# Two levels of the seven-product scheme in the last ten MLP blocks, and weights read twice instead of once

## The chip, the cores and the metric

The kernel runs on one core of a Trainium2 chip. The metric is the device time of one execution in microseconds (us). Engines are named as in the profile: PE is TensorE's matmul side, PEld its weight loads, DVE is VectorE, ACT is ScalarE, POOL is GpSimd, and SP issues DMAs.

## The reference

The core computes attention with a threshold and, on its result, a two-layer MLP with an exact GELU:

```python
# q, k, v: (8, 8, 576, 64) float32
scale = 1.0 / np.sqrt(q.shape[-1])
scores = scale * np.matmul(q, k.transpose(0, 1, 3, 2))
thresh = np.max(scores, axis=-1, keepdims=True) - tau
scores = np.where(scores >= thresh, scores, -1000000000.0)
scores = scores - np.max(scores, axis=-1, keepdims=True)
attn = np.exp(scores)
attn = attn / (np.sum(attn, axis=-1, keepdims=True) + 1e-09)
x = np.matmul(attn, v)            # then (B, H, S, D) -> (B*S, H*D): 4608 tokens x 512
...
h = x @ w_in                      # w_in: 512 x 2048
g = 0.5 * h * (1.0 + erf(h / sqrt(2)))
out = g @ w_out                   # w_out: 2048 x 512
```

The two weight matrices arrive as 64-bit floats: `setup_inputs` multiplies a float32 array by a 64-bit scalar. The kernel turns them into 32-bit floats on the chip.

## The kernel before

**Work and its units.** Attention is done by pairs of heads: 32 pairs, each in five steps ("slots") of up to 128 query rows. The MLP is done by blocks of 256 tokens, 18 in all. Blocks 0 to 7 ("plain", `PLAIN`) are computed as written. Their matmuls are laid into the attention slots by `fill`, which emits as many of them as a hand-set curve (`GOAL`) says. Every instruction stands in its engine's queue in the order in which the program emits it (`manual_schedule`), and an engine executes its queue in order.

**The early phase.** The first 20 slots treat the four head pairs of the first batch. In them the weights are converted as well. `load_piece` fetches one piece of 128 x 512 64-bit numbers (512 KB). `conversions` turns a piece into 32-bit floats with two ACT and three DVE instructions: L172 and L173 on ACT, L180, L182 and L184 on DVE. There are 32 pieces. `convert(ns)` emits conversion steps until their nominal lengths (the numbers after `yield`) use up the budget of the slot, 3800 from the fourth slot on. A conversion that ends fetches the next piece, so a few pieces are under way at any time: half of them land in the halves of `turned_p`, which the early phase doesn't need yet, half in free buffers of x.

**The tail.** The last ten blocks, 8 to 17, are left to the end of the program (`strassen`). They are treated two at a time ("duos"), by the scheme that computes a 2 x 2 block matrix product with seven products in place of eight. For layer one the four blocks of x are the two 256-token blocks by the two halves of the 512 inputs, and w_in is cut in 2 x 2. For layer two the four blocks of the hidden values are again the two token blocks by the two halves of the 2048 hidden values. The sums of weights that the scheme needs are built on DVE before the tail (`weights_in`, L628 to L636), the sums of x for each duo in `x_sums` (L654 to L657), and those of the hidden values in `finish_chunk` (L711 to L713). Each product of layer one is two matmuls of 256 columns; all matmuls of the tail stand on line L688 (`product`). A product that has been accumulated in a PSUM bank is copied by ACT or added by DVE to a tile in SBUF, and the next product may be accumulated on top of it in the same bank only when that has been done. Between the last chunk of layer one and the matmuls of layer two that need its sums stands a short seam; layer two of a duo keeps all its sums in PSUM over the 1024 hidden values of a half, eight matmuls to a product.

**Blocks put away.** Blocks 8 to 12 are finished before the tail begins, so `put_away` writes them to DRAM and `bring` reads them back during the tail. Blocks 13 to 17 stay in SBUF; the first duo is (13, 14). The last head pair's result is divided by the softmax sums on POOL (`divide`, L502) just as the tail begins.

Of the kernel before, what the change touches and what calls it, by code (L numbers as in the profile page):

```python
# [8 lines left out]
FP32 = mybir.dt.float32  # L9
# [9 lines left out]
def kernel(  # L19
# [28 lines left out]
    nc = tc.nc  # L48
# [22 lines left out]
    order = list(range(PLAIN + 5, N_BLK)) + AWAY  # L71
    DUOS = list(zip(order[0::2], order[1::2]))
# [6 lines left out]
    ld = ctx.enter_context(tc.tile_pool(name="ld", bufs=2))  # L79
    work = ctx.enter_context(tc.tile_pool(name="work", bufs=2))  # L80
    one = ctx.enter_context(tc.tile_pool(name="one", bufs=1))
    small = ctx.enter_context(tc.tile_pool(name="small", bufs=4))
    xg = ctx.enter_context(tc.tile_pool(name="xg", bufs=7))
    op = ctx.enter_context(tc.tile_pool(name="op", bufs=2))
    gp = ctx.enter_context(tc.tile_pool(name="gp", bufs=N_DF // 2 + 2))
    dg = ctx.enter_context(tc.tile_pool(name="dg", bufs=1))
    dram = ctx.enter_context(tc.tile_pool(name="dram", bufs=1, space=bass.MemoryType.DRAM))
    ps = ctx.enter_context(tc.tile_pool(name="ps", bufs=4, space=PSUM))

# [8 lines left out]
    q_tail = [const.tile([P, P], FP32, name=f"q_tail{i}") for i in range(4)]  # L98
    v_sb = [const.tile([P, 2, KR, D], FP32, name=f"v{i}") for i in range(4)]

    turned_p = const.tile([P, 2, 2, 4 * KR, 2 * Q], FP32, name="turned_p")
    pd = [turned_p[:, e, :, :, :].rearrange("p h b i -> p (h b i)") for e in range(2)]
    sums = [const.tile([P, Q], FP32, name=f"sums{i}") for i in range(2)]
    for t in sums:
        nc.vector.memset(t, 1.0)
    pd_tail = [const.tile([P, 4 * KR, Q], FP32, name=f"pd_tail{i}") for i in range(2)]
# [7 lines left out]
    w_in_sb = [const.tile([P, d_ff], FP32, name=f"w_in{c}") for c in range(N_DM)]  # L114
    w_out_sb = [const.tile([P, d_model], FP32, name=f"w_out{j}") for j in range(N_DF)]
# [20 lines left out]
    def load_piece(eng=nc.gpsimd):  # L136
        k = loaded[0]
        if k == len(pieces):
            return
        staged = k % 2 and k < len(pieces) - LATER  # L140
        dst, src = pieces[k]
        loaded[0] += 1
        if not wide:
            nc.sync.dma_start(dst, src)
            converted[0] += 1
            load_piece()
            return
        if staged:

            half, at = divmod(k // 2 % 4, 2)  # L150
            raw = pd[half].bitcast(U32)[:, at * 2 * PIECE:(at + 1) * 2 * PIECE]
        else:
            raw = xg.tile([P, 2 * PIECE], U32, tag="x", name="raw")
        eng.dma_start(raw, src.bitcast(U32))
        raws.append((dst, raw))

    def conversions():
# [9 lines left out]
        while raws or ahead:  # L167
            if raws:
                dst, raw = raws.pop(0)
                lo, hi = (raw.rearrange("p (f w) -> p f w", w=2)[:, :, i] for i in range(2))  # L170
                power = gp.tile([P, PIECE], U32, tag="g", name="power")
                nc.scalar.activation(power.bitcast(FP32), hi.bitcast(FP32), AF.Copy, bias=0.0, scale=2.0 ** -112)  # L172
                nc.scalar.activation(dst.bitcast(U32), lo, AF.Copy, bias=0.0, scale=2.0 ** -29)  # L173
                ahead.append((dst, hi, power))
                yield 0
            if len(ahead) == LATER and converted[0] == len(pieces) - LATER:
                yield None
            if len(ahead) == 2 or not raws:
                dst, hi, power = ahead.pop(0)
                vec.tensor_scalar(power, power, 3, 0x7FFFFFF8, op0=ALU.logical_shift_left, op1=ALU.bitwise_and)  # L180
                yield 340
                vec.scalar_tensor_tensor(power, hi, 0x80000000, power, op0=ALU.bitwise_and, op1=ALU.bitwise_or)  # L182
                yield 720
                vec.tensor_tensor(dst.bitcast(U32), power, dst.bitcast(U32), op=ALU.add)  # L184
                load_piece()
                converted[0] += 1
                yield 640
# [45 lines left out]
    def load_early(p):  # L233
        b, hp = divmod(p, HP)
        s = st[p] = {}
        for name, src in (("q", q), ("k", k)):

            pool, tag = (xg, "x") if p == 2 else (ld, name)
            t = s[name] = pool.tile([P, 2, NC + 1, D], FP32, tag=tag, name=name)
# [17 lines left out]
    def turn_qk_early(p):  # L257
# [24 lines left out]
        for j, name in enumerate("qk"):  # L282
            t = s.pop(name)
            for e in range(2):
                nc.tensor.matmul(tr[e * D:(e + 1) * D, j, 0:TAIL], lhsT=t[0:TAIL, e, NC, :],
                                 rhs=ident[0:TAIL, 0:TAIL], start=True, stop=True)
        nc.scalar.copy(kT[:, S:S + TAIL], tr[:, 1, 0:TAIL])
# [176 lines left out]
    def weigh_v(p, lo, hi):  # L464
# [16 lines left out]
        for n, o, at, size in in_blocks(b, lo, hi):  # L481
            if n not in x_blk:
                x_blk[n] = xg.tile([P, N_DM, TOK], FP32, tag="x", name="x")
# [59 lines left out]
    def block_steps(n):  # L543
# [3 lines left out]
        for j in range(N_DF):  # L547
# [8 lines left out]
            if j % 2:  # L556
                late.append((g, j, hT))
                gelus(lag[0])
        for m in range(TOK // P):
# [42 lines left out]
    HF = d_ff // 2  # L602
    NJ = HF // P
    HD = d_model // 2
    NK = HD // P
    U = 512
    vec = nc.vector

    def units(t):
        flat = t.rearrange("p a b -> p (a b)") if len(t.shape) == 3 else t.rearrange("p a b c -> p (a b c)")  # L610
        return [flat[:, k * U:(k + 1) * U] for k in range(flat.shape[1] // U)]

    def unit(pool, tag, n=1):
        t = pool.tile([P, n, U], FP32, tag=tag, name="unit")
        return [t[:, k, :] for k in range(n)]

    def weights_in():

        room = [x for tag in ("q", "k", "qT", "kT") for _ in range(2) for x in unit(ld, tag)]
        room += unit(work, "p", 2) + unit(work, "p", 2)  # L620
        x_ext = [units(v_sb[i % 4])[0].rearrange("p (c t) -> p c t", c=NK) for i in range(NP - 4, NP - 1)]
        s1, s2, s4 = ({} for _ in range(3))
# [338 lines left out]
```

## Time and profile before

| | before |
|---|---|
| median of 3 runs | 1383.6 us (1381.98 to 1385.34) |
| the profiled execution's own time | 1385.34 us |
| its span, first to last instruction | 1383.6 us |
| mean granted TensorE clock | 0.994 |
| busy: PE, PEld, DVE, ACT, POOL | 1363.2, 970.0, 884.1, 654.1, 413.7 us |
| tail: first matmul of L688 to the end of the last | about 892.9 to 1380.5 us |

The profiled execution takes 1.7 us more outside its span, and it is the slowest of the three runs, 1.7 us over the median. Busy time is the time in which an engine has an instruction in work; matmuls overlap their neighbours, so PE's busy share says little of how well it is used. The chain of waits follows back from the last instruction to whatever released each step.

### The profile page before, as it was taken

The numbers are of one execution on the slowest core, as the hardware profiler recorded it, in microseconds if no ns is written. First come the engines' busy times: TensorE is split into PE (matmuls) and PEld (weight loads), VectorE is DVE, ScalarE is ACT, GpSimd is POOL, SyncE is SP. The second block draws the span as 40 slices with busy tenths as digits, with TensorE's granted clock in tenths as the row PEclk, the third lists the DMA queues.
The fourth block names the chain that finished last, engine by engine and source line by source line (L and its number), as shares of the span: only waits on it lengthen the run. The fifth ranks groups of instructions, "written<-read, shape, count | busy, mean of one in ns | idle before, by whom it ended". The sixth has DMA issues, their size and how long they took to land.

```text
span 1383.6 us, 20244 instructions
## 1 busy us (share of the span) xinstructions
PE 1363.2 (99%) x6734; PEld 970.0 (70%) x6734; DVE 884.1 (64%) x1707; ACT 654.1 (47%) x1192; POOL 413.7 (30%) x864
## 2 busy tenths in 40 slices
PE   8899999999999999999999999999999999999999
PEld 6577557466466466466476475588888888888887
DVE  6987677788888888888888888764142232241330
ACT  7886537457457448358367366241140230330420
POOL 4331344455555554554555551100000000000000
PEclk9999999999999999999999999999999999999999
DMA  9741266667777777787787776500000001001000
GB/s 273 193 143 34 66 153 150 143 152 180 152 172 183 156 189 177 158 202 175 160 207 167 165 186 122 112 0 8 23 1 24 22 1 46 16 0 54 9 8 23
DMA packets 212406, 152.43 MB, mean 110 GB/s; under 512 B 113664, under 2 KB 198976, under 8 KB 212304
## 3 DMA queue, kind: packets, MB, share of 16 engines
q1 hardware_dynamic: 191040, 112.84, 36.0%
q0 software_dynamic: 20832, 38.01, 9.8%
q8 instruction: 55, 0.90, 0.3%
q14 instruction: 47, 0.39, 0.1%
q10 hardware_dynamic: 432, 0.30, 0.1%
HBM read 55.97 MB, written 12.52 MB: 49 GB/s over the span
## 4 chain that ended last, share of the span: by engine, by line
PE 95%; DVE 2%; ACT 2%; issue 1%; DVEq 0%; ACTq 0%
PE bank L688 35%; PE o_ps L568 17%; PE hT L554 16%; PE sc L362 13%; PE xT L479 11%; PE tr L304 2%; DVE power L182 1%; DVE nmx L374 1%; ACT p L377 0%; DVE p L393 0%; ACT power L172 0%; DVE power L180 0%; ACT pT L312 0%; PE idle L122 0%; ACT diag L407 0%
## 5 line engine op out<-in xcount | busy, mean ns | idle before, releaser
L377 ACT ACTIVATE p<-sc,nmx 128x576 f32<-128x576 f32 x288 | 202.1, 738 | 273.0 <-DVE nmx L374 272.9
L393 DVE SCALAR_TENSOR_TENSOR p<-sc,thr,p 128x576 f32<-128x576 f32 x288 | 225.3, 816 | 60.5 <-ACT p L377 58.9
L374 DVE TENSOR_REDUCE nmx<-sc 128x1 f32<-128x576 f32 x288 | 205.6, 751 | 72.4 <-PE sc L362 71.7
L554 PE MATMUL hT<-x,w_in 128*128 128x256 f32 x1024 | 241.1, 385 | 0.0
L568 PE MATMUL o_ps<-w_out,g 128*128 128x512 f32 x512 | 239.0, 608 | 0.0
L554 PEld LDWEIGHTS hT<-x,w_in 128*128 128x128 f32 x1024 | 189.5, 190 | 49.2 <-issue 23.5
L375 POOL TENSOR_SCALAR thr<-nmx,tau_eff 128x1 f32<-128x1 f32 x288 | 87.8, 305 | 407.2 <-DVE nmx L374 406.2
L568 PEld LDWEIGHTS o_ps<-w_out,g 128*128 128x128 f32 x512 | 93.9, 191 | 112.0 <-issue 110.4
L479 PE MATMUL xT<-pT,v 128*64 128x256 f32 (+1 forms) x1280 | 163.8, 409 | 0.1
L362 PE MATMUL sc<-kT,qT 64*128 64x288 f32 x960 | 157.6, 433 | 3.2 <-DVE p L393 2.6
L440 DVE STREAM_TRANSPOSE turned_p<-p 128x1152 f32<-128x1152 f32 x112 | 154.4, 1378 | 3.9
L362 PEld LDWEIGHTS sc<-kT,qT 64*128 64x128 f32 x960 | 90.1, 188 | 76.6 <-issue 64.4
L479 PEld LDWEIGHTS xT<-pT,v 128*64 128x64 f32 x1280 | 89.1, 137 | 72.2 <-issue 13.6
L688 PE MATMUL bank<-x,w_in 128*128 128x256 f32 x480 | 116.7, 379 | 0.0
L688 PE MATMUL bank<-w_out,unit 128*128 128x256 f32 x520 | 115.5, 379 | 0.0
L229 POOL DMA_DIRECT2D v<-in_v_dram x208 | 110.8, 536 | 4.6 <-issue 2.7
L688 PEld LDWEIGHTS bank<-w_out,unit 128*128 128x128 f32 x520 | 98.8, 190 | 13.4
L688 PEld LDWEIGHTS bank<-x,w_in 128*128 128x128 f32 x480 | 91.2, 190 | 12.8 <-issue 0.5
L688 PE MATMUL bank<-v,unit 128*128 128x256 f32 x320 | 82.1, 379 | 0.0
L220 POOL DMA_DIRECT2D q<-in_q_dram x104 | 70.8, 686 | 8.5 <-issue 8.1
L688 PE MATMUL bank<-unit,turned_p 128*128 128x256 f32 x320 | 73.1, 379 | 0.0
L540 ACT ACT_TABLE_LOAD x56 | 71.8, 1283 | 1.0
(156 smaller groups left out, 1476.2 us busy)
## 6 DMA issues: line engine op xcount, KB each, us to landing
pT<-turned_p SPq DMA_DIRECT2D x448, 160.0 KB, 3.6
pT<-pd_tail SPq DMA_DIRECT2D x112, 80.0 KB, 2.9
q<-in_q_dram POOLq DMA_DIRECT2D x104, 72.0 KB, 3.4
k<-in_k_dram POOLq DMA_DIRECT2D x104, 72.0 KB, 2.9
inv<-turned SPq DMA_DIRECT2D x56, 128.0 KB, 3.9
v<-in_v_dram POOLq DMA_DIRECT2D x156, 40.0 KB, 3.2
x<-x SPq DMA_DIRECT2D x10, 512.0 KB, 4.4
raw<-in_moe_w_out_dram POOLq DMA_DIRECT2D x9, 512.0 KB, 4.1
```

Source lines behind the costliest of these rows:

```text
L229: eng.dma_start(t[r:P:4, e, 0:n, :], rows[:, r * KR:r * KR + n, :])
L362: nc.tensor.matmul(sc[e][:, h, 0:HALF], lhsT=lhsT, rhs=s["kT"][rows, at:at + HALF], start=True, stop=True)
L374: nc.vector.tensor_reduce(nmx[:, e:e + 1], sc, axis=AXIS.XY, op=ALU.max, negate=True)
L375: nc.gpsimd.tensor_scalar(thr[:, e:e + 1], nmx[:, e:e + 1], -1.0, tau_eff, op0=ALU.mult, op1=ALU.subtract)
L377: nc.scalar.activation(w[:, e * S:(e + 1) * S].rearrange("p (h s) -> p h s", h=2), sc, AF.Exp, bias=nmx[:, e:e + 1], scale=1.0)
L393: nc.vector.scalar_tensor_tensor(row, sc[e][:, :, 0:HALF], thr[:, e:e + 1], row, op0=ALU.is_ge, op1=ALU.mult, accum_out=den[e])
L440: nc.vector.transpose(turned_p[:, :, i // 2, 0:NB, i % 2 * Q:(i % 2 + 1) * Q], w.rearrange("p (e b i) -> p e b i", e=2, i=Q))
L479: nc.tensor.matmul(to, lhsT=s["v"][:, e, c, :], rhs=rhs, start=(c == 0), stop=(c == KR - 1))
L540: nc.scalar.activation(warm[:, 1:2], warm[:, 0:1], AF.Exp)
L554: nc.tensor.matmul(hT[:, j % 2, :], lhsT=w_in_sb[c][:, j * P:(j + 1) * P], rhs=x_blk[n][:, c, :], start=(c == 0), stop=(c == N_DM - 1))
L568: nc.tensor.matmul(o[:, 0:d_model], lhsT=g[j][:, m * P:(m + 1) * P], rhs=w_out_sb[j], start=(j == 0), stop=(j == N_DF - 1))
L688: nc.tensor.matmul(to, lhsT=l, rhs=r, start=start and k == 0, stop=k == len(pairs) - 1, skip_group_check=not start)
```

## The change

**Tail.** The ten blocks are treated in two groups of five, 1280 tokens at a time. Layer one applies the seven-product scheme twice, one inside the other: every one of the seven outer products (a quarter of w_in's sums by a quarter of x's sums) is itself seven products of 128 inputs, 128 hidden values and 320 tokens, one matmul of 320 columns each. That makes 49 matmuls for one chunk of 512 hidden values, and there are four chunks (`NJ = 4`). Layer two stays one level deep, and is computed for each chunk as soon as that chunk's hidden values are there; its result is added up in SBUF over the four chunks. The sums that the inner level needs are built for each chunk on POOL, beside the matmuls; the sums of x come on DVE and POOL.

**Conversion.** A piece is fetched twice, the second time shifted by three bytes, and converted by one ACT and four DVE instructions. Two pieces rather than four are fetched at the start, and one rather than two in each of two later places. The nominal lengths add up to 2100 a piece where they added up to 1700.

**Storage.** x's seven buffers, w_in and w_out become one tile each, and the pools are closed and reopened so that the tail's tiles take the place of attention's.

The core of the diff:

```diff
             if raws:
-                dst, raw = raws.pop(0)
-                lo, hi = (raw.rearrange("p (f w) -> p f w", w=2)[:, :, i] for i in range(2))
+                dst, raw, shifted, slots = raws.pop(0)
+                hi = raw.rearrange("p (f w) -> p f w", w=2)[:, :, 1]
+                top = shifted.rearrange("p (f w) -> p f w", w=2)[:, :, 0]
                 power = gp.tile([P, PIECE], U32, tag="g", name="power")
-                nc.scalar.activation(power.bitcast(FP32), hi.bitcast(FP32), AF.Copy, bias=0.0, scale=2.0 ** -112)
-                nc.scalar.activation(dst.bitcast(U32), lo, AF.Copy, bias=0.0, scale=2.0 ** -29)
-                yield 0
+                vec.tensor_scalar(power, hi, 0x7FF00000, None, op0=ALU.bitwise_and)
+                nc.scalar.activation(power, power, AF.Relu, bias=rebias, scale=8.0)
+                yield 340
...
-                vec.tensor_scalar(power, power, 3, 0x7FFFFFF8, op0=ALU.logical_shift_left, op1=ALU.bitwise_and)
+                vec.tensor_scalar(mant, top, 0x0FFFFFFF, 0x10000000, op0=ALU.bitwise_and, op1=ALU.bitwise_or)
                 yield 340
                 vec.scalar_tensor_tensor(power, hi, 0x80000000, power, op0=ALU.bitwise_and, op1=ALU.bitwise_or)
                 yield 720
-                vec.tensor_tensor(dst.bitcast(U32), power, dst.bitcast(U32), op=ALU.add)
+                vec.scalar_tensor_tensor(dst, mant, 2.0 ** -28, power.bitcast(FP32), op0=ALU.mult, op1=ALU.mult)
                 load_piece()
-                yield 640
+                yield 700
...
         eng.dma_start(raw, src.bitcast(U32))
+        n = 8 * PIECE - 4
+        eng.dma_start(shifted.bitcast(U8)[:, 0:n], src.bitcast(U8)[:, 3:3 + n])
...
+    def taken(to, x, first):
+        if first is None:
+            nc.scalar.copy(to, x)
+        else:
+            add(vec, to, first, x)
+    def step(which):
+        if which is not None:
+            which()
+        if beside:
+            beside.pop(0)[1]()
+        while beside and beside[0][0] is pool:
+            beside.pop(0)[1]()
+    def chain(n, m, takes, done=None, runs=1):
+        x, y = bank("sc", n), bank("mm", n)
+        v = bank("mm", n) if "m2" in m else None
...
+        before = waiting.pop(0) if waiting else (None, None)
+        step(one_of("m1", x, True))
+        step(before[0])
+        step(one_of("m7", y, True))
+        if v is not None:
+            step(one_of("m2", v, True))
+        step(before[1])
+        step(one_of("m6", x, False))
+        step(one_of("m4", y, False))
+        waiting.append((one_of("m5", x, False), one_of("m3", x, False)))
...
+        R, U, V, W, T = c[:, 0], c[:, 1], c[:, 2], c[:, 3], g[:, 0]
+            takes = {"m1": [at(0, 0)], "m7": [at(1, 1)], "m6": [at(1, 0)], "m4": [at(1, 0, True)],
+                     "m2": [at(0, 0, True)], "m5": [at(1, 1, True)], "m3": [at(0, 1)]}
...
+        def m5_all():
+            m5_out(0, 1)()
+            add(pool, flat(U), flat(U), flat(T))
+        def sums(t):
+            g11, g21, g12, g22 = (z[:, :, t, :] for z in (R, U, V, W))
+            sub_first = g[:, 0, :, t, :], g[:, 1, :, t, :]
+            add(vec, sub_first[0], g21, g22)
+            sub(vec, sub_first[1], sub_first[0], g11)
+            sub(vec, g21, g11, g21)
+        outer("a11", "b11", R, None)
+        outer("s1", "t1", T, None)
+        between()
+        outer("s2", "t2", U, R)
+        outer("s3", "t3", V, U, when(m2=m5_out(0, 0), m4=m5_out(1, 0), m5=m5_out(1, 1), m3=m5_all))
+        outer("a12", "b21", R, R, when(m3=lambda: (gelu_on(flat(W)), gelu_on(flat(R)))))
+        outer("a22", "t4", V, V, when(m3=lambda: gelu_on(flat(V))))
+        last = {"m2": lambda: gelu_on(U[:, 0, 0, :]), "m4": lambda: (gelu_on(U[:, 1, 0, :]), sums(0)),
+                "m5": lambda: gelu_on(U[:, 1, 1, :]), "m3": lambda: (gelu_on(U[:, 0, 1, :]), sums(1))}
+        outer("s4", "b22", U, U, when(**last))
+    def layer_out(blocks, j, between):
...
+        before = waiting.pop(0)
+        for m in range(MT):
+            v = bank("mm", HD)
+            def run(m=m, v=v):
+                product(v, rows(g12, m, w(1, 0)), True)
+                taken(lo[m][:, 0:HD], v, None if first else lo[m][:, 0:HD])
+            step(run)
+            if m < 2:
+                step(before[m])
+        between(-1)
+        beside.insert(0, (vec, lambda: sub(vec, g12, g12, gs2)))
+        for m in range(MT):
...
+            chain(HD, ms, takes, done)
+            between(m)
+    def last_blocks():
+        x_tiles()
+        beside.extend(x_sums())
+        for _ in range(9):
+            beside.pop(0)[1]()
+        w_out_sums(pool, 0)
...
+                if m == -1:
+                    if after[0] != n:
+                        for b, x in enumerate(GROUPS[after[0]]):
+                            nc.sync.dma_start(xall[:, b, :, :], away.pop(x))
+                    w_in_sums(pool, after[1])
+                if m == 1 and after[0] != n:
+                    beside.extend(x_sums())
```

In it, `x`, `y` and `v` are PSUM banks, two buffers for `x` and four shared by `y` and `v`; `g11`, `g21`, `g12` and `g22` of layer two are R, U, V and W, and `gs1`, `gs2` the two halves of `g`. `HD` is 256, `MT` is 5, and `w_in_sums` is 16 POOL instructions over 5632 columns for a chunk, run on DVE for the very first chunk. `x_sums` is 28 subtractions of 320 columns and four, the outer ones, of 1280.

## The prediction, made before the result was known

> **What bounds the kernel now.** I read the page first: busy shares and the chain that ended last.
>
> ```profile
> PE 1363.2 (99%) x6734; PEld 970.0 (70%) x6734; DVE 884.1 (64%) x1707; ACT 654.1 (47%) x1192; POOL 413.7 (30%) x864
> PE bank L688 35%; PE o_ps L568 17%; PE hT L554 16%; PE sc L362 13%; PE xT L479 11%; PE tr L304 2%; DVE power L182 1%; DVE nmx L374 1%; ACT p L377 0%; DVE p L393 0%; ACT power L172 0%; DVE power L180 0%; ACT pT L312 0%; PE idle L122 0%; ACT diag L407 0%
> ```
>
> PE carries the chain; the tail (L688) is 35% of it. Busy time by stretches shows two stages with different limits.
>
> ```profile
> 35.00:70.00 35.00, 28.38 (x200) 20.66 (x200) 32.96 (x70) 31.17 (x66) 13.38 (x26) 0.90 0.69 192
> 105.00:140.00 35.00, 34.51 (x212) 26.36 (x213) 24.73 (x54) 23.68 (x53) 6.10 (x17) 1.00 0.17 32
> 1000.00:1100.00 100.00, 99.48 (x462) 87.25 (x461) 29.37 (x70) 26.08 (x67) 0.00 (x0) 1.00 0.05 16
> ```
>
> Columns: the stretch, its length, then PE, PEld, DVE, ACT, POOL busy with instructions, granted clock, DMA share, GB/s. Around 50 us DVE is full (33.0 of 35), the only place where the weight conversion can matter. In the tail PE is full and DVE 29% busy: there a matmul saved is time saved, as long as its results are taken from PSUM in time. The chain in order of time prices the matmuls.
>
> ```profile
> 349.18 3.63 PE o_ps L568 x8
> 450.86 4.49 PE o_ps L568 x10
> 725.34 3.65 PE hT L554 x16
> 801.35 4.08 PE hT L554 x18
> 941.08 96.97 PE bank L688 x448
> ```
>
> A float32 matmul is two records. Two more records of 512 columns cost 0.86 us, of 256 columns 0.43. One matmul is thus 0.432 at 256 (96.97/224 agrees), 0.86 at 512, and, on the line between, 0.538 at 320. From the groups by shape come the other prices (last numbers: busy us, mean ns).
>
> ```profile
> L735 DVE TENSOR_TENSOR v<-v,bank 128x256 f32<-128x256 f32 x10 | 4.2, 421 | 3.7 <-PE bank L688 3.7
> L629 DVE TENSOR_TENSOR unit<-unit,w_in 128x512 f32<-128x512 f32 x4 | 2.8, 691 | 0.1
> L527 ACT ACTIVATE g<-g 128x512 f32<-128x512 f32 x6 | 3.2, 618 | 0.0
> L739 ACT ACTIVATE turned_p<-turned_p 128x256 f32<-128x256 f32 x10 | 4.2, 416 | 4.5 <-DVE turned_p L738 4.5
> L502 POOL TENSOR_TENSOR x<-x,inv 128x256 f32<-128x256 f32 x40 | 28.6, 728 | 0.0
> L502 POOL TENSOR_TENSOR x<-x,inv 128x128 f32<-128x128 f32 x16 | 7.3, 457 | 0.0
> L180 DVE TENSOR_SCALAR power<-power 128x512 uint32<-128x512 uint32 x32 | 13.5, 421 | 6.2 <-ACT power L172 6.2
> ```
>
> On straight lines a DVE add takes 0.49 at 320 columns, 0.82 at 640, 1.49 at 1280. The next one starts 0.08 before its end if independent, 0.04 to 0.08 after it if it needs the result (starts in the timeline). A GELU takes 0.47 at 320 and about 1.2 at 1280; POOL takes 0.86, 1.27 and 2.9 at 320, 512 and 1280. The timeline (start, length, idle before and what ended it) prices a product that must wait for a bank.
>
> ```profile
> 1038.08 0.42 DVE L738 TENSOR_TENSOR turned_p<-turned_p,bank 128x256 f32<-128x256 f32 x1 [0.44 <-PE bank L688]
> 1038.56 1.13 PE L688 MATMUL bank<-x,unit 128*128 128x256 f32 x4 [0.52 <-DVE turned_p L738]
> ```
>
> DVE starts 0.2 after the last column, PE 0.06 after DVE's end, and the first record then takes 0.1 longer (1.13 us for four where others show 1.03). Five such seams, one a duo, cost 0.8 each, 3.9 in all: 1120 x 0.432 + 3.9 = 487.7, the tail's measured 487.5.
>
> **Matmuls saved.** Layer one falls from 7 x 2 x 8 x 5 = 560 matmuls of 256 columns (241.9 us) to 49 x 4 x 2 = 392 of 320 (210.9): **31.0 us less**. Layer two keeps 14 x 5 x 4 x 2 = 560 of 256. The tail without stalls is 452.8.
>
> **Stalls in each chunk.** In the middle of a chunk DVE keeps up: one add of 0.41 to 0.49 for each product of 0.538. At the seam it doesn't. I walk the three queues from the end of product m4 of the last outer product s4 (t = 0), the time in us, for a chunk that isn't its group's first:
>
> - ACT: the GELU of V waits for m3 of the outer product before (its matmul ends at -1.08, DVE's add at -0.4) and runs to 0.85. PE's next product, v of m = 0, reads V and starts at 0.91. **Idle 0.91.**
> - The GELU of U's (1,0) ends at 1.38. DVE has already started on `sums(0)`, which stands next in its queue and waits for that: 1.42 to 3.8 (three adds of 640). Only then come v's add (4.15) and that of m5 (4.56). PE finished m5 and the second v at 3.28 and may accumulate m3 into m5's bank at 4.62. **Idle 1.34.**
> - m3 is added by 5.96, its GELU ends at 6.49, `sums(1)` at 8.9, three adds of v at 9.95, that of layer two's first m1 at 10.29. PE ended m7 at 9.58 and starts m6 in m1's bank at 10.35. **Idle 0.78.**
> - V minus gs2 (1280 columns) runs to 11.7, m7's add to 12.04; PE, done at 11.32, starts m4 at 12.10. **Idle 0.78.** From here DVE has one add of 0.34 for each 0.86.
>
> With 0.1 for each restart that is 4.2 us. In a group's first chunk ACT takes the v's, and only the first idle and 1.0 of the second are left: 2.1. Together 6 x 4.2 + 2 x 2.1 = **29.4**.
>
> **Stalls at the ends.** At the start w_in's sums (5632 columns at 1.04 ns and 16 starts of 0.11: 7.7 us from 879.8) and the first nine sums of x keep DVE until PE ends the plain blocks at 892.9, as L628 to L657 did; m1 has nothing to wait for. But `t3` is POOL's, behind the division (to 894.7) and four adds of w_out (5.0) and takes 2.9: 902.6. DVE reaches its sums of t3 at 900 with m5's add behind them, and PE waits 6.3. Between the groups x's sums delay two more products, 2.1, if the five blocks return within 12 us (2.6 MB; 273 GB/s in the first slice gives 9.6 plus some 2). The last m3 waits for m5: 0.8. The last store is two DMAs, not one: 0.4. **9.6** together.
>
> **POOL beside DVE.** In the trace of before, POOL's small add at L396 takes 0.24 alone and 0.89 beside a DVE instruction with two SBUF inputs, which keeps its 0.69 (timeline again):
>
> ```profile
> 12.37 0.24 POOL L396 TENSOR_SCALAR den<-den 128x2 f32<-128x2 f32 x1 [1.50 <-DVE p L393]
> 52.35 0.89 POOL L396 TENSOR_SCALAR den<-den 128x2 f32<-128x2 f32 x1 [1.41 <-DVE p L393]
> 52.18 0.69 DVE L184 CUSTOM_DVE_ANT_0 w_in<-power,w_in 128x1024 uint16<-128x1024 uint16 x1
> ```
>
> So I let POOL be the one that waits. Its sums for the next chunk (5632 columns, 14 us) have 30 us of layer two to hide in, even at twice the time; only the first t3 is exposed: 2 us more. DVE slowed in return is not seen: I take 0, and one POOL add of about 1 us before each of four DVE sums, 8 x 4 = 32, as the other end.
> The Trainium skill's page "GPSIMD Engine Reference" (Specifications) says POOL's SBUF interfaces are shared with DVE, in contention with DVE instructions "in a 2-port perf mode or with two SBUF inputs". It speaks against moving sums to POOL beside `sums(1)`; it doesn't say who waits. The rows show POOL waiting; by the rule read the other way the sum would be that other end.
>
> **Conversion.** DVE per piece now: L180, L182, L184 start 0.45, 0.72 and 0.61 apart, 1.79. After: two masks at 0.35 (if their strided inputs run like L180; 0.61 if like L182), 0.61 and 0.73: 2.04 to 2.56. A slot's budget of 3800 holds 2.2 pieces before (4.0 us) and 1.8 after (3.7 to 4.6). Around 50 us a slot lasts 6.8, full of DVE; over 12 such slots that is -3.6 to +8. The rest of the pieces falls where DVE has room (24.7 of 35 busy). ACT sheds a 0.68 us instruction a piece. DMA: 1.8 MB a slot of 6.8 us is 266 GB/s beside q, k and v, where 273 GB/s made the DMAs 90% busy in the first slice; waits of up to 6 are possible, and DVE's softmax stands behind a late piece. I take **+1**, ends -4 and +14.
>
> **Sum.** Against the profiled execution's own 1385.3: tail 452.8 + 29.4 + 9.2 = 491.4 against 487.5, +3.9; store +0.4; t3 +2; conversion +1: 1392.6. The median of the runs is 1.7 lower: **1391**, 0.5% slower.
>
> **Rivals.**
> - *DVE keeps up at the seam* (faster). The walk hangs on queue order and three extrapolated lengths. For it: DVE needs some 22 of the 26 us of layer one, so the work fits on the average. Against it: the order is fixed, and DVE waits for ACT ahead of PE's adds. Without the 29.4 the time is 1362. The sign turns when a chunk's stalls average below 2.7 in place of 3.7. Chance 0.22.
> - *DVE held by POOL at the seam* (slower): the other end above, 1391 + 32 = 1423 in full, half of it 1407. For it: no row has a long POOL add beside such a sum. Against it: the 0.69 beside L396. Chance 0.13.
> - *The conversion binds*: +14 in place of +1, 1404. For it the DMA share, against it the smaller budget. Chance 0.15.
> - *The sums don't run beside the products*: if products wait for writers of other parts of the same large tile (x, c), PE waits for POOL's 25 us a chunk; a fifth of it is 40 us, over 1430. No row speaks for it. Chance 0.05.
>
> **How the numbers follow.** Forecast 0.45. 0.2% (2.8 us) is about what a measurement can tell from no change. Faster: nearly all of the first rival, 0.20, and 0.03 of the forecast's lower edge. Same: 0.10, from the forecast. Slower: 0.67. The range leaves out the deeper half of the first rival and most of the second and fourth: 1372 to 1412. The forecast's own range is 1382 to 1400.
>
> **What would show it.** Right: no more idle in layer one's middle than 0.1 a product; PE idle behind "ACT" before a v product (0.9), behind DVE before m3 (1.3), m6 and m4 (0.8 each) in chunks two to four; 320-column matmuls 0.538 apart; the tail 491 long; its start near 893. Wrong: two-input DVE sums longer than 0.82, the tail's start later than 897, or DVE level at m3.

## The result and the profile after

| | before | after |
|---|---|---|
| median of the runs | 1384.0 us (1382.0 to 1385.3) | 1432.7 us (1431.6 to 1434.2) |
| the profiled execution's own time, its span | 1385.3, 1383.6 | 1431.6, 1429.8 |
| tail: first matmul to the end of the last | 892.9 to 1380.5 = 487.5 | 888.1 to 1425.1 = 537.1 |
| matmul time of the tail at full pace | 483.8 | 452.8 |
| PE's time over that pace | 3.7 | 84.3 |

The changed kernel takes 1.0354 times as long, with an interval of 1.0336 to 1.0372; forecast were 1391 us, with a range of 1372 to 1412. The last row is the difference of the two above it. Where a wait is priced "over the pace" below, the spacing of the tail's matmul records is set against the nominal one (0.216 at 256 columns, 0.270 at 320): whatever is over it is waiting or a slow clock. The matmuls shrank by 31.0 us as forecast. The time over the pace grew by some 80.

The page of the kernel after, first the busy times, then the chain by line:

```profile
PE 1353.3 (95%) x6398; PEld 911.7 (64%) x6398; DVE 1106.9 (77%) x2040; ACT 600.2 (42%) x1000; POOL 683.4 (48%) x1106
PE bank L781 27%; PE o_ps L611 16%; PE hT L596 14%; PE sc L403 12%; PE xT L520 10%; DVE c L663 2%; DVE g L663 2%; ACT c L834 1%; DVE o L666 1%; PE tr L345 1%; DVE g L666 1%; DVE x L663 1%; DVE c L666 1%; DVE p L434 1%; DVE nmx L415 1%
```

The tail's matmuls now stand on L781, and behind them the chain has DVE's sums (L663, L666), which it didn't have before. The same stretches as in the prediction, with the same columns:

```profile
35.00:70.00 35.00, 30.31 (x216) 22.20 (x215) 34.24 (x76) 25.48 (x52) 18.50 (x35) 0.95 1.04 324
1000.00:1100.00 100.00, 92.62 (x383) 73.69 (x382) 64.38 (x123) 10.80 (x20) 38.68 (x34) 0.97 0.00 1
```

In the tail DVE went from 29% to 64% busy, POOL from nothing to 39%, and PE from 99% to 93% at a clock of 0.97. Around 50 us it is the other way round: PE got busier. The groups of DVE's instructions in the tail say where to look (last numbers: busy us, mean ns of one):

```profile
L666 DVE TENSOR_TENSOR c<-c,bank 128x320 f32<-128x320 f32 x304 | 147.3, 487 | 40.0 <-PE bank L781 27.1
L663 DVE TENSOR_TENSOR g<-g,c 128x640 f32<-128x640 f32 x16 | 26.5, 1655 | 0.6
L663 DVE TENSOR_TENSOR c<-c 128x640 f32<-128x640 f32 x16 | 24.2, 1511 | 0.0
L663 DVE TENSOR_TENSOR c<-c,g 128x1280 f32<-128x1280 f32 x8 | 15.0, 1880 | 0.0
```

An add of a bank to a tile takes the 0.49 that the line through before's rows gave. An add of 640 columns with both inputs in SBUF takes 1.66 and 1.51 in place of 0.82. That was the first sign under "Wrong" in the prediction. The timeline of DVE and POOL at one seam shows why (start, length, idle before):

```profile
1057.95 1.78 DVE L663 TENSOR_TENSOR g<-g,c 128x640 f32<-128x640 f32 x1
1059.65 1.88 DVE L663 TENSOR_TENSOR c<-c 128x640 f32<-128x640 f32 x1
...
1057.19 1.85 POOL L663 TENSOR_TENSOR s_out<-w_in,s_out 128x512 f32<-128x512 f32 x1
1059.12 1.73 POOL L666 TENSOR_TENSOR s_in<-s_out 128x512 f32<-128x512 f32 x1
1060.92 1.73 POOL L663 TENSOR_TENSOR s_in<-s_in,s_out 128x512 f32<-128x512 f32 x1
```

The two engines take turns. DVE's sum starts while POOL's is under way and ends 0.7 us after POOL's end; POOL's next starts in the middle of DVE's and is stretched in its turn, from 1.27 to 1.73. A still plainer pair stands at the change of groups, where some 0.45 us of DVE's work stood beside one long instruction of POOL:

```profile
1149.69 3.07 DVE L663 TENSOR_TENSOR x<-t_x 128x320 f32<-128x320 f32 x1
...
1149.52 2.88 POOL L663 TENSOR_TENSOR xall<-xall 128x1280 f32<-128x1280 f32 x1 [14.30 <-DMA out_dram<-o]
```

What that does to PE, at the same seam:

```profile
1062.31 0.81 PE L781 MATMUL bank<-xall,s_in 128*128 128x320 f32 x2 [3.06 <-DVE c L666]
1062.95 5.30 PE L781 MATMUL bank<-w_out,c 128*128 128x256 f32 x16
1068.09 1.03 PE L781 MATMUL bank<-t_out,c 128*128 128x256 f32 x4
1069.66 1.13 PE L781 MATMUL bank<-t_out,g 128*128 128x256 f32 x4 [0.54 <-DVE o L666]
1071.97 1.13 PE L781 MATMUL bank<-t_out,c 128*128 128x256 f32 x4 [1.18 <-DVE o L666]
```

The lines with idle time are m3, m6 and m4. m3 waits 3.06 us, and the sixteen records behind it take 5.30 us: the granted clock is 0.5 for 3.4 us. The last chunk has no sums of a next chunk beside it, and is a control that the kernel brings with it:

```profile
1393.38 0.81 PE L781 MATMUL bank<-xall,s_in 128*128 128x320 f32 x2 [1.01 <-DVE c L666]
1394.02 3.62 PE L781 MATMUL bank<-w_out,c 128*128 128x256 f32 x16
1397.48 1.03 PE L781 MATMUL bank<-t_out,c 128*128 128x256 f32 x4
1399.05 1.13 PE L781 MATMUL bank<-t_out,g 128*128 128x256 f32 x4 [0.54 <-DVE o L666]
1400.78 1.13 PE L781 MATMUL bank<-t_out,c 128*128 128x256 f32 x4 [0.60 <-DVE o L666]
```

There the waits are those of the walk: by the spacing 1.13 (the v product), 1.27, 0.81 and 0.87 us, where the walk, with 0.1 for each restart, had 1.01, 1.44, 0.88 and 0.88. The two other long waits stand at the tail's start and between the groups, both behind DVE:

```profile
904.95 1.44 PE L781 MATMUL bank<-xall,s_plain 128*128 128x320 f32 x2 [11.89 <-DVE c L666]
1154.21 1.13 PE L781 MATMUL bank<-w_out,c 128*128 128x256 f32 x4 [3.18 <-DVE o L666]
```

### The profile page after: what moved, and what is told of

It is laid out like the page before. It is cut to its first block, busy times and chain, and to the rows that moved or that the text cites. A ratio compares the mean times of both kernels' runs of the same rounds, so it can differ in the third digit from the quotient of the medians.

```text
span 1429.8 us, 20064 instructions
## 1 busy us (share of the span) xinstructions
PE 1353.3 (95%) x6398; PEld 911.7 (64%) x6398; DVE 1106.9 (77%) x2040; ACT 600.2 (42%) x1000; POOL 683.4 (48%) x1106
## 4 chain that ended last, share of the span: by engine, by line
PE 80%; DVE 12%; ACT 3%; DMA 2%; issue 1%; SPq 1%; POOL 0%; ACTq 0%; DVEq 0%; POOLq 0%
PE bank L781 27%; PE o_ps L611 16%; PE hT L596 14%; PE sc L403 12%; PE xT L520 10%; DVE c L663 2%; DVE g L663 2%; ACT c L834 1%; DVE o L666 1%; PE tr L345 1%; DVE g L666 1%; DVE x L663 1%; DVE c L666 1%; DVE p L434 1%; DVE nmx L415 1%
## 5 line engine op out<-in xcount | busy, mean ns | idle before, releaser
L415 DVE TENSOR_REDUCE nmx<-sc 128x1 f32<-128x576 f32 x288 | 205.5, 750 | 62.5 <-PE sc L403 61.7
L596 PE MATMUL hT<-xall,w_in 128*128 128x256 f32 x1024 | 241.1, 385 | 0.0
L596 PEld LDWEIGHTS hT<-xall,w_in 128*128 128x128 f32 x1024 | 189.5, 190 | 49.2 <-issue 23.9
L666 DVE TENSOR_TENSOR o<-o,bank 128x256 f32<-128x256 f32 x240 | 98.4, 418 | 106.8 <-PE bank L781 105.8
L666 DVE TENSOR_TENSOR c<-c,bank 128x320 f32<-128x320 f32 x304 | 147.3, 487 | 40.0 <-PE bank L781 27.1
L781 PE MATMUL bank<-w_out,c 128*128 128x256 f32 x480 | 131.7, 409 | 12.0 <-ACT c L834 6.9
L781 PEld LDWEIGHTS bank<-w_out,c 128*128 128x128 f32 x480 | 98.3, 207 | 35.9 <-ACT c L834 10.9
L834 ACT ACTIVATE c<-c 128x320 f32<-128x320 f32 (+1 forms) x56 | 44.6, 811 | 141.4 <-DVE c L666 73.1
L792 ACT COPY c<-bank 128x320 f32<-128x320 f32 x32 | 13.6, 426 | 196.9 <-PE bank L781 196.8
L663 POOL TENSOR_TENSOR t_out<-w_out 128x512 f32<-128x512 f32 x16 | 21.5, 1345 | 146.2 <-PE bank L781 146.2
L781 PE MATMUL bank<-t_out,c 128*128 128x256 f32 x320 | 84.9, 389 | 6.5 <-DVE o L666 6.5
```

What stands on the lines that cost most here:

```text
L415: nc.vector.tensor_reduce(nmx[:, e:e + 1], sc, axis=AXIS.XY, op=ALU.max, negate=True)
L596: nc.tensor.matmul(hT[:, j % 2, :], lhsT=w_in_sb[c][:, j * P:(j + 1) * P], rhs=x_blk[n][:, c, :], start=(c == 0), stop=(c == N_DM - 1))
L663: eng.tensor_tensor(out, a, b, op=ALU.subtract)
L666: eng.tensor_tensor(out, a, b, op=ALU.add)
L781: nc.tensor.matmul(to, lhsT=l, rhs=r, start=start and k == 0, stop=k == len(pairs) - 1, skip_group_check=not start)
```

## The experiments

The first theory was: DVE's two-input sums are held by POOL's, and PE's long waits bring a half clock that costs as much again. The rivals: DVE simply has too much work at the seam; or the start and the change of groups carry the loss. Gains are read against the median of 1432.7. The cuts of the edits are shortened, and comments in them are for the reader.

**e1 and e2: POOL's sums away from the seam.** In e1 POOL's sums for the next chunk wait until `V` minus `gs2` is done:

```diff
-                if m == -1: ... w_in_sums(pool, after[1])
+                if m == 0:
+                    pool.tensor_copy(tail["sp"][:, 0, 0, 0:1], tail["c"][:, 2, 0, 0, 0:1])
+                    w_in_sums(pool, after[1])
```

> The kernel after, but POOL's sums of w_in for the next chunk start only when DVE has taken gs2 from V (POOL first copies one column of V). Theory H (a DVE instruction with two SBUF inputs waits until POOL's running add ends, and the other way round): the three-add sums at the seam return from 1.5 to 1.7 us an add to 0.82, every seam looks like that of the last chunk, which has no POOL sums beside it (1.0, 1.2, 0.7, 0.8 us idle), no idle reaches 3 us, and the half clock behind the seams is gone: about 4 us less in each of seven chunks, some 28 us, 1404. Rival S (the sums are slow because their operands lie in strides of 320 columns): the adds keep 1.5 us and more, time within 5 us of 1433. A third way: POOL's 20 us end too late for the next chunk and part of the gain goes there.

In e2 the same 16 sums are done by DVE, one behind each product, and POOL has none:

```diff
-                    w_in_sums(pool, after[1])
+                    w_in_sums(Later(), after[1])     # each op: beside.append((vec, op))
```

> The kernel after, but the 16 sums of w_in for the next chunk go to DVE, one behind each of 16 products of layer two, and POOL has none. Theory H: seams as in the last chunk, 1404 as in the run with POOL held; DVE has 0.5 us free for each product of 0.86 there and the sums take 0.2 to 0.7, so a few tenths of idle a chunk at most. Rival S: the seams stay as they were, and DVE has 8 us more to do in each chunk: 1433 or more.

Measured: 1405.9 us (1.0151 of before, 1.0136 to 1.0166) and 1405.6 (1.0147, 1.0130 to 1.0165). The groups of e1:

```profile
L663 DVE TENSOR_TENSOR g<-g,c 128x640 f32<-128x640 f32 x16 | 13.2, 825 | 0.6
L663 DVE TENSOR_TENSOR c<-c 128x640 f32<-128x640 f32 x16 | 13.1, 817 | 0.0
L663 DVE TENSOR_TENSOR c<-c,g 128x1280 f32<-128x1280 f32 x8 | 11.9, 1481 | 0.0
```

The sums are back at 0.82 and 1.48, and the eight seams (over the nominal pace) fall from 61.7 to 28.7 us. The median falls by 27: the profiled execution of e1 has its tail's start 4.8 us later than that of the kernel after, and its change of groups takes 3 more. Two opposite ways to part the engines give the same time, so neither the work nor its place on POOL is the cause, but that both run at once. In e2 DVE did these 16 sums of each chunk on top of its own at 3 us more in the seams than e1 and 2 less between the groups; it has room.

**e3: the conversion alone**, put into the kernel before.

> The kernel before, with the conversion of the kernel after (two fetches a piece, one ACT and four DVE instructions, two pieces fetched at the start) and nothing else of the change. The kernel after stands 9 us ahead of the one before at 400 us. Theory: that is the conversion, which takes 0.7 us less of ACT and no more of DVE in each full slot; time 1375. Rival: it comes of the other storage of x and the pools, or the ends of the early phase move and are lost again by the curve that lays out the MLP; time 1384.

1380.0 us, 0.9971 of before (0.9959 to 0.9982): the conversion gains 4.5 us, between the two values.

**e12: the ACT instruction put back into e3**, to see why it gains.

```diff
                 nc.scalar.activation(power, power, AF.Relu, bias=rebias, scale=8.0)
+                lo = raw.rearrange("p (f w) -> p f w", w=2)[:, :, 0]
+                nc.scalar.activation(dst.bitcast(U32), lo, AF.Copy, bias=0.0, scale=2.0 ** -29)
```

> The kernel of e3 (the one before with only the new conversion, 1380.0), with the second ACT instruction of a piece put back (0.68 us, 32 times; what it writes is overwritten by DVE's mask). Theory (the conversion gains because ACT is the engine that PE waits for around 50 us: PE's waits for ACT's diag fell from 7.7 to 5.3 us and the half-clock windows from five to two): the time goes back to that of before, 1384 or a little more, and PE waits for ACT's diag 7 us or more. Rival (the gain comes from fewer pieces fetched at once or from another share of the slots): 1380, as e3.

1384.5 us, 1.0007 of before (0.9994 to 1.0019): all of the gain is gone. The stretch around 50 us, first of e3, then of e12 (that of before is in the prediction: DVE 32.96, ACT 31.17):

```profile
35.00:70.00 35.00, 28.64 (x209) 20.88 (x207) 33.00 (x76) 24.63 (x52) 17.86 (x34) 0.90 1.01 307
```

```profile
35.00:70.00 35.00, 28.31 (x198) 19.97 (x199) 32.06 (x72) 29.99 (x62) 17.30 (x34) 0.90 1.01 299
```

DVE is about equally full in all three, and ACT goes 31.2, 24.6, 30.0. So the gain hangs on the second ACT instruction of a piece. Whether by ACT's load or by DVE's mask, which in e12 has to wait for that instruction because both write the same tile, this run doesn't tell. Through which waits it reaches PE is no clearer: PE waited 6.4 us for ACT's `diag` in e3, 7.3 in e12 and 7.7 before (the 5.3 of the expectation is that of the kernel after), and e12 has 13.6 us at half clock where e3 has 6.8.

**e4: a clock test**, in the kernel before: 0, 2, 4, 7 and 10 extra DVE copies at its five seams, so that PE idles for graded times.

```diff
+                if j == NJ - 1:
+                    for _ in range((0, 2, 4, 7, 10)[sb]):
+                        vec.tensor_copy(gs1(j), x)
```

> The kernel before, with 0, 2, 4, 7 and 10 extra DVE copies out of the waiting bank at the five seams between layer one and layer two, so that PE is idle there for about 0.8, 1.4, 2.1, 3.2 and 4.2 us. Theory C (an idle of PE of about 3 us brings half the TensorE clock for some 3.4 us): matmul records 0.42 apart in place of 0.216 behind the fourth and fifth seam only, 1.7 us lost behind each; time about 1384 + 8 + 3.4 = 1395. Rival (the half clock in the kernel after comes of its load, or of POOL and DVE at work, and not of the idle): records 0.216 apart behind every seam, 1392.

1397.2 us (one run). PE's timeline at the third and the fourth seam:

```profile
1136.86 1.13 PE L688 MATMUL bank<-x,unit 128*128 128x256 f32 x4 [2.22 <-DVE turned_p L742]
1137.83 1.46 PE L688 MATMUL bank<-w_out,unit 128*128 128x256 f32 x6
```

```profile
1237.42 1.34 PE L688 MATMUL bank<-x,unit 128*128 128x256 f32 x4 [3.60 <-DVE turned_p L742]
1238.56 4.71 PE L688 MATMUL bank<-w_out,unit 128*128 128x256 f32 x14
```

Behind 2.22 us of idling six records take 1.46; behind 3.60 fourteen take 4.71, some of them twice as long as the rest: 1.5 us more than fourteen at full pace. The longest wait, 5.1 us, has the same behind it. So in this kernel idling does bring the half clock (other runs, at the end of this document, say when), and one spell of it costs up to 1.7 (5.30 against 3.62 for sixteen records at after's seam).

**e5 and e9: PE kept running through m3's wait** by five spare matmuls of 256 columns. The lines are those of e9; e5 writes to `tail["other"]` in place of `nxt`.

```diff
+            if m == 1:
+                for _ in range(5):
+                    nc.tensor.matmul(nxt, lhsT=w_out_sb[0][:, 0:P], rhs=w_out_sb[0][:, 0:HD], start=True, ...)
```

> The kernel after, with five spare matmuls of 256 columns (2.16 us, into an unused half of a PSUM bank, never read) put in front of the product m3 that waits 3.2 us at each seam of layer one. No other instruction moves. Theory (after an idle time of about 3 us PE runs at half clock for 3.4 us): the wait falls to about 1 us, the half-clock windows behind the eight seams go (30.7 us at half, 15 us of work lost), 1432.7 - 15 = about 1418. Rival (the records 0.42 apart are a price of the adds that hold the seam, not of PE's idling): the spare matmuls change nothing, 1433.

1465.5 us (1.0590, 1.0573 to 1.0608): no test of the clock. The spare matmuls went into the other half of a bank tile that DVE still had to read, waited 2.8 to 3.1 us for it, and then ran their 2.2 to 3.6 us on top.

> As e5, but the five spare matmuls of each seam go into the bank that the third v product of layer two overwrites next, so that they wait for nothing that DVE still has to do (in e5 they waited 2.8 us for DVE themselves and added their own time). Theory (half clock follows an idle time of about 3 us): the wait of m3 falls from 3.2 to about 1, the half-clock windows behind the seams go, about 1418. Rival (the 0.42 apart belong to the adds and not to PE's idling): no gain, 1433 or more.

1442.1 us (1.0425, 1.0410 to 1.0439). Here they did what they were meant to; PE's timeline at one seam:

```profile
997.11 2.32 PE L920 MATMUL bank<-w_out 128*128 128x256 f32 x10
1000.35 0.81 PE L781 MATMUL bank<-xall,s_in 128*128 128x320 f32 x2 [0.92 <-DVE c L666]
1000.99 3.62 PE L781 MATMUL bank<-w_out,c 128*128 128x256 f32 x16
1004.44 1.03 PE L781 MATMUL bank<-t_out,c 128*128 128x256 f32 x4
1007.71 1.13 PE L781 MATMUL bank<-t_out,g 128*128 128x256 f32 x4 [2.24 <-DVE o L666]
1010.01 2.07 PE L781 MATMUL bank<-t_out,c 128*128 128x256 f32 x4 [1.17 <-DVE o L666]
```

m3 waits 0.92, and the sixteen records behind it run at full pace (3.62). But m6 now waits 2.24 where it waited 0.54: PE comes 1.7 us earlier to the same add, which DVE ends no sooner. Counted from the seam's first v product, m6 and m4 start at 12.97 and 15.27 us here, and at 12.95 and 15.26 at after's seam shown above (1056.71). The half clock behind m3 had thus cost nothing there; DVE's queue covered it. The second half of the first theory falls. The kernel became slower because the long idle time now lies before m6 and m4, and the half clock behind m4, where no wait for DVE covers it: this seam takes 11.3 us over the pace where it took 8.4, and the eight together some 69 in place of 61.7. The trace of after has one such seam by itself, at 1324 to 1340 us: full pace behind m3, m6 waiting 2.24, half clock behind m4, 11.4 us in all.

**e6: the start**, on e1. `t3` on DVE, `t4` behind the sums of `t3`, POOL's sums of w_out behind its sums of x.

```diff
-        yield from outer(pool, part["b12"], part["b22"], part["b12"])
-        yield from outer(vec, t4, part["b21"], t2)
...
-        yield from inner(vec, "t2", t2)
+        yield from inner(vec, "t2", t2, True)
+        yield from outer(vec, part["b12"], part["b22"], part["b12"])
         yield from inner(vec, "t3", part["b12"])
+        yield from outer(vec, t4, part["b21"], t2)
...
```

> The kernel with POOL's sums held back at the seam (1405.9), and with the sums of x in another order: t3 on DVE behind the sums of t2, t4 behind those of t3, and POOL's four sums of w_out for the first chunk behind its sums of x. Theory (PE's 11.9 us at the tail's start and its 9 us at the change of groups are DVE standing behind POOL's adds and behind t3, and 6.9 and 1.7 of them half clock behind the idle): the start falls to 5 to 8 us of short waits with no half clock, the change of groups to about 4: about 1389. Rival (DVE and POOL simply have more sums there than PE leaves time for): 1400 or more.

1395.3 us (1.0080, 1.0065 to 1.0095). The change of groups fell from 10.1 to 4.5 us over the pace, as expected, but the start only from 14.2 to 10.6, in two waits of 4.6 and 2.6 us, each still with half clock behind it. (The expectation counted 6.9 us of half clock at the start; by the spacing it was 2.5.)

**e7: the seam's order**, on e1. `a22` ahead of `a12`, each GELU as soon as its sum is there, `sums(0)` behind the adds of v and m5, the second half's sums one at every second product.

```diff
-        outer("a12", "b21", R, R, when(m3=lambda: (gelu_on(flat(W)), gelu_on(flat(R)))))
-        outer("a22", "t4", V, V, when(m3=lambda: gelu_on(flat(V))))
+        outer("a22", "t4", V, V, when(m4=lambda: gelu_on(flat(W)), m3=lambda: gelu_on(flat(V))))
+        outer("a12", "b21", R, R, when(m3=lambda: gelu_on(flat(R))))
...
-                "m4": lambda: (gelu_on(U[:, 1, 0, :]), sums(0)), "m5": lambda: gelu_on(U[:, 1, 1, :]),
-                "m3": lambda: (gelu_on(U[:, 0, 1, :]), sums(1))
+                "m4": lambda: gelu_on(U[:, 1, 0, :]), "m5": lambda: (gelu_on(U[:, 1, 1, :]), sums0()),
+                "m3": lambda: gelu_on(U[:, 0, 1, :])      # sums(1): beside, one op, one empty step
```

> The kernel with POOL's sums held back (until V minus gs2, as there), and with another order at the seam: the outer product a22 (V) before a12 (R), so that V and W have their GELU early; sums(0) behind the adds of v and m5; the second half's sums and V minus gs2 in two halves, one of them at every second product of layer two. Nothing is removed. Theory (the 3.65 us of each seam are the order of ACT's and DVE's queues): nearly all of them go, 7 x 3.65 + 2 = about 27 less than 1405.9, 1379. Rival (DVE has no room there, the waits only move to later products): 1395 or more.

1382.5 us (0.9993, 0.9981 to 1.0005). PE's seam, and a stretch of windows, of e7:

```profile
1043.86 1.03 PE L781 MATMUL bank<-w_out,c 128*128 128x256 f32 x4
1044.72 0.70 PE L781 MATMUL bank<-xall,s_in 128*128 128x320 f32 x2
1045.26 1.03 PE L781 MATMUL bank<-w_out,c 128*128 128x256 f32 x4
1046.12 0.70 PE L781 MATMUL bank<-xall,s_in 128*128 128x320 f32 x2
1046.66 3.62 PE L781 MATMUL bank<-w_out,c 128*128 128x256 f32 x16
```

```profile
985.00:1035.00 50.00, 50.00 (x214) 40.19 (x213) 32.69 (x71) 6.44 (x13) 22.27 (x24) 1.00 0.00 1
```

No idle time is left there: the eight seams together are 4 us over the pace in place of 28.7. It is the same work in another order; only one subtraction of 1280 columns a chunk is cut in two. A part came back elsewhere: the change of groups takes about 13 us over the pace in place of e1's 10.1, and the start 15.1 in place of 14.2.

**e8, e10, e11: everything together**, with the blocks' buffers chosen so that ACT doesn't copy into one whose write to memory is under way (it waited for two, 3.0 and 2.5 us, near 605 and 709).

> The two changes of order together, with sums held back, and with buffers for blocks 9 to 15 chosen so that none is used while it is still being written to memory (3.0 and 2.5 us of PE waiting near 606 and 709 us, with some half clock). Theory: the savings add up, 17 + 27 + 4 from 1405.9: about 1358, below both kernels. Rival (one stage's slack is the other's cover): over 1370.

1379.9 us (0.9971, 0.9961 to 0.9982) where 1358 was expected: the start kept 14.1 us and the change of groups about 10. PE waits twice at the start, 4.5 us up to 900 (DVE's add stands behind sums of x that waited for the division) and 5.2 us up to 920. POOL's timeline shows what is ahead of the second:

```profile
903.20 0.86 POOL L665 TENSOR_TENSOR xall<-xall 128x320 f32<-128x320 f32 x1 [9.60 <-DVE t_x L665]
```

POOL's sums of `b21` overwrite what `t4` reads, and `t4` had moved to the end of DVE's queue, so POOL idled 9.6 us and was then late for its adds for W, for which DVE waits 5.9 us. In e10 the order is mended:

```diff
+        w_out_sums(pool, 0)                # in weights_first, before the last division
...
+        yield from rest(7 if at_start else 0)
         yield from outer(vec, t2, part["b22"], t1)
         yield from outer(vec, t4, part["b21"], t2)
+        yield from inner(pool, "b21", part["b21"])
+        yield from inner(pool, "t4", t4)
...
+        yield from rest(15 if at_start else 0)
+        yield from inner(pool, "b22", part["b22"])
```

> As e8, with the tail's start in yet another order: the first chunk's sums of w_out on POOL ahead of the last division, where POOL idles 16 us; no sums of x in DVE's queue during the first outer product; t4 ahead of the sums of t2; POOL's sums of b21 and t4 behind t4, those of b22 after its adds for W and U. In e8 PE waited 4.7 us at 895 (DVE's sums of x, queued ahead of its adds, stood behind the division) and 5.4 us at 914 (POOL's sums, queued ahead of its adds for W, stood behind t4, whose input they overwrite), each with half clock behind it. Theory: both go, to 2 to 4 us of short waits: 1380 - 13 = about 1367. Rival (the work of the start doesn't fit beside 26 us of PE): 1376 or more.

1372.2 us (0.9922, 0.9908 to 0.9937); the start is down to 8.2. e11 adds empty steps behind `t2`, `t4` and `t3`:

> As e10, with the sums of x spread out further: t1 ahead of the sums of b11, an empty step behind each of t2, t4 and t3, and t4 behind the sums of t2. In e10 PE still waited 4.5 us at 897 (DVE's add for T behind t2, t4 and two sums beside POOL's) and 3.6 us at 1116 (DVE's sums beside POOL's sums of w_in), each with half clock behind it. Theory (DVE's adds come late because two or more sums of 1280 columns stand ahead of one add): the wait at 897 falls under 2 us, and the half clock behind it goes; the one at 1116 loses 1 us: 1372 - 5 = about 1367. Rival (POOL's adds beside set DVE's pace there, whatever the order): 1371 or more.

1368.7 us (0.9884, 0.9866 to 0.9902), 1.2% under the kernel before and 4.5% under the kernel after. Its windows beside the one above:

```profile
1000.00:1100.00 100.00, 100.00 (x412) 77.19 (x410) 69.19 (x149) 17.96 (x30) 43.04 (x42) 1.00 0.04 14
```

Its tail takes 473.1 us, 452.8 of matmuls and 20.1 over: 5.9 at the start, 9.0 between the groups.

## Why the prediction was wrong, point by point

Set against the profiled execution (1431.6 where the sum gave 1392.6; times over the nominal pace):

| term | forecast | measured |
|---|---|---|
| eight seams | 29.4 | 61.7 |
| start, with t3's 2 | 8.3 | 14.5 |
| between groups | 2.1 | 7.1 |
| last m3 | 0.8 | 0.8 |
| tail's start (892.9 before) | +1 | -4.8 |
| from the tail's end to the end of the execution (4.9 before) | +0.4 | +1.6 |

The first four rows measure the tail by its spacing, 84.1 in all (84.3 in the table further up). The differences add up to 32.3 + 6.2 + 5.0 - 5.8 + 1.2 = 38.9 of the 39.0.

- **The step that failed** is "DVE slowed in return is not seen: I take 0". What the runs showed in its place: beside POOL the sums of 640 columns take 1.66 and 1.51 in place of 0.82, and the seams 32.3 us more than the walk; with POOL's sums held back (e1) or on DVE (e2) this is gone, so the cause is shown. The other end, 32, named the mechanism, but that its size fits is in part luck: it counted 4 us at each of eight seams. Against e1, six seams lost 3.7 to 4.9, the seventh 7.2 with a long half clock behind m4, and the last, which has no POOL sums beside it, nothing.
- **Why the row couldn't carry that 0.** At L396 a POOL add came while a DVE instruction was under way, and the one that came second waited. At the seam POOL's adds run without a break, so DVE is the second one as often. "Not seen" meant that no row had a long POOL add already running when a DVE sum started; the end that no row excluded deserved more than 0.13. The Trainium skill's page "SBUF — State Buffer" (section "Who interferes with whom") says that a DVE instruction with two SBUF inputs contends with a GpSimd instruction that reads SBUF, that the shared ports are an exclusive lock, and that the order of issue decides who blocks. The runs agree, in both directions: 0.82 to 1.66 on DVE, 1.27 to 1.85 on POOL.
- **The walk of the seam was right.** Without POOL beside it, the seam of a chunk that isn't the first takes 4.1 (forecast 4.2) and that of a group's first chunk 2.0 (2.1), in e1 and in after's last chunk. e7 shows that the cause is the order of the queues, as the walk had it. The rival "DVE keeps up" didn't happen in this kernel; the seams of e7 are what it would have been.
- **Prices of matmuls, adds and GELUs held**: 0.54 and 0.43 a matmul, 0.487 an add with one input in PSUM (beside POOL too), 0.82 and 1.48 for two in SBUF alone, 0.47 and 1.27 a GELU (0.47 and 1.2).
- **The other rivals**: in after's list of waits PE waits for DVE and ACT and never for POOL, so the products did run beside the sums; and the conversion didn't bind.
- **Start: mis-sized**, 14.5 for 8.3. The wait was the one named (DVE behind the division, w_out's sums and `t3`), but the two outer sums took 5.0 us beside POOL's in place of 3, and the sums behind them stood behind `t3`; 2.3 is half clock. Between groups it was the same hold (the 3.07 above).
- **Conversion: wrong sign**, a gain of 4.5 (e3) in place of +1. It was counted on DVE's budget alone; ACT's shed instruction was mentioned and priced at nothing, and e12 shows that the gain hangs on it. The tail's start in one profile is a rough measure, though: among kernels with the same early phase it lies between 888.1 and 893.1. The 4.8 is also net of ACT's two waits for buffers on their way to memory (5.5 us, of which 2.3 reach PE by its list of waits), which the prediction didn't look for among the changes of storage.
- **Half clock: not foreseen** and visible (16.9 us by the spacing), but e9 shows that behind m3 it lay in DVE's shadow, at the seam compared. It counts at the start and where m6 and m4 wait long.

What stays open: how much of the change of groups (9.0 in e11) is POOL's hold and how much the four sums of 1280 columns ahead of single adds; and whether ACT's instruction costs by its length or by the wait of DVE's mask, and through which waits it reaches PE.

## What to carry to other kernels

When work moves to POOL, list what DVE does beside it with two inputs in SBUF, and price both engines as taking turns, instruction by instruction; adds that read PSUM are free of it. Saved matmuls become saved time only when the takers' queues are ordered for them: here one order costs 24 us more of waiting at the seams than another with the same work (e1 and e7), 23 us of the median. At the seams here (after and e9) a slow clock behind a wait was a cost only where PE, and not the engine it waited for, was late at the next meeting.

## What the runs showed of the hardware

- POOL and DVE hold each other for whole instructions: a DVE add of 320 columns took 3.07 us beside a POOL add of 2.88. With one input in PSUM it takes 0.487 either way: in the kernel after, 211 such adds beside a long POOL add and 93 without one have the same mean.
- PE's clock falls to half by windows. In each trace the spells of half clock start whole multiples of 3.413 us apart (at 998.41, 1063.26 and 1128.11 in after, 19 windows from one to the next), and they last one or more windows. Let the tails of all fourteen traces be cut into such windows, and the time be added up in each in which PE has no record at work. Of the windows at full clock, 41 were followed by half clock, and each had 1.96 us or more of idling; all the others had 1.95 or less. So a wait counts by how it lies. The first of the two below was split by a boundary into 1.9 and 1.5 and left the clock alone (e7). The second is shorter, lay inside one window and brought the half clock (e11). The wait of 3.06 that ends at 1327 in after was split like the first.

```profile
1128.06 1.13 PE L781 MATMUL bank<-w_out,c 128*128 128x256 f32 x4 [3.42 <-DVE o L666]
1119.08 2.08 PE L794 MATMUL bank<-w_out,c 128*128 128x256 f32 x4 [2.42 <-DVE o L668]
```

- The Trainium skill's page "TensorE: Matmul & The Clock Gate" (Part 1) has windows of 3.4 us that run freely, which agrees; it gives one idle window as what brings the half clock, where these tails show some 1.95 us of idling inside one. By that page's formula, half of the time at half clock, after's 47.8 us would cost an estimated 24; the spacing shows 16.9, since PE also idled in them, and part of that was covered.
